# Attention and two feed-forward blocks on one core: planner prices for the later blocks, w_in's first chunk in another place, w_out asked for later, sums of the last pass freed from its scale

## The chip, the cores and the metric

The kernel runs on one core of a Trainium2 chip. The metric is the device time of one execution in microseconds (us). TensorE does the matrix products, VectorE and ScalarE the elementwise work and the evacuation of PSUM, GpSimd some elementwise sums, and SyncE (SP) asks for all transfers.

## The reference

```python
# q, k, v: [4, 8, 768, 64] f32; mem_k, mem_v: [4, 8, 8, 64]
for c in range(24):                       # chunks of 32 queries
    ctx = rows c*32-16 .. c*32+32+8       # cut at both ends of the sequence
    k_full, v_full = concat(mem, ctx)
    s = q_c @ k_full.T / 8
    out[c] = softmax(s) @ v_full          # sum + 1e-9 below
x = out.transpose(0, 2, 1, 3).reshape(3072, 512)
h = x @ w_in                              # 512 x 2048
g = max(h, 0) + alpha * min(h, 0)
y = g @ w_out                             # 2048 x 512
result = ((y @ w_a) * (y @ w_b)) @ w_o2   # 512 x 1536 twice, 1536 x 512
```

The weights come as 64-bit floats, the rest as 32-bit.

## The kernel before, in words

The tokens are cut into 24 attention units of 128 tokens. Seven blocks follow: two of two units (256 tokens), then five of four units (512 tokens). For each block the kernel computes attention into `x32`, finds its largest size, forms a scale by powers of two (`scale`), and splits x into a high and a low 16-bit half (`split_hi` on ScalarE, L347; `split_lo` on VectorE, L351) in `xhl`. A product of two split operands is three 16-bit products (`gemm3`, L910 to L912). `gemm1` makes 16 tiles of g and splits them into `ghl`, `gemm2` makes four tiles of y and stores them to `yd` in HBM.

The weights are turned from words of 64-bit floats into 32-bit floats by bit operations on VectorE (`chunk`, L537 to L560, with an absolute value on ScalarE, L531), scaled and split. w_in comes in eight chunks of 256 columns, with one scale for all of them (`scale_w1`: the maximum over all chunks at L495, the result `s_w1`). Its raw words lie in places that are free then: chunk 0 in the place of `xhl`, chunks 1 to 3 in that of `ghl`, the rest in that of w_out's halves. w_out comes in eight chunks of 64 columns, whose raw words take turns in the three places of `raw_slots`. w_a, w_b and w_o2 come in six chunks each (a "pair" chunk); they are summed into the seven operands of a two-by-two fast product, split, and written to HBM (`spill`).

x's scale (`x_block`, L877 finds the block's largest value) reads s_w1, because one of the two products formed behind it, `iy`, contains w_in's inverse scale.

The second half (`second`) runs six passes of 512 tokens. A pass computes y's two products for six pairs of columns by seven products each (`pair`, `quarters`), multiplies them, and takes the largest size (`amp`). When all six pairs are done, one scale is formed over them (L1253 to L1258), `operands` makes the four sums of each pair's product (`sums`, L367, on GpSimd, or on VectorE in the last pass), splits the seven operands, and `output` makes two tiles of tokens by seven products over all six pairs.

The order of the work is a plan. Every instruction group is put into a list with `sd.op(engine, cost, rank, ...)`: its engine (or a choice of engines), its price in us (`dve`, `act`, `pe`, `pool`, `dma`, or numbers), a rank, and the tiles it reads and writes. `Schedule.emit` then simulates the engines with these prices: at each step it takes the group that can start first, the lower rank where two can start at the same time, and issues it. Each engine and SP's queue then keep that order on the chip, whatever the real durations are. Places (`Slots`) are given out in the same simulation; unless a class of places is marked otherwise, its users take places in the order in which they were declared. An attention unit's transfers have the rank twice its number (unit 3, the fourth, has 6.0), w_out's chunks 4.1, 4.6, 5.1 and so on.

Of the kernel before, what the change touches and what calls it, by code (L numbers as in the profile page):

```python
# [172 lines left out]

def dve(n, rate=1.04, pointers=0):
# [16 lines left out]
def tile_attention_moe_moe2(  # L191
# [28 lines left out]
    TB = 512  # L220
    EARLY = 8
# [82 lines left out]
    def scale(amax, s, inv, reads, writes, rank=-2000, after=()):  # L304


        ps = Buf(mm_slots)

        def across():
            nc.tensor.transpose(out=ps.tile[:, :P], in_=amax().to_broadcast([P, P]), identity=ident)  # L310

        m = Buf(m_slots)

        def largest():
            nc.vector.tensor_reduce(out=m.tile, in_=ps.tile[:, :P], axis=AX.X, op=ALU.max)
# [12 lines left out]
        sd.op("PE", pe(P, 2), -9000, across, reads, [(ps, 0)])  # L328
        sd.op("DVE", dve(P), rank, largest, [(ps, 0)], [(m, 0)])
        sd.op("DVE", 0.07, rank, power, [], [(m, 0)])  # L330
        sd.op("DVE", 0.07, rank, inverse, [(m, 0)], [(m, 1)])
        last = [(m, 2)] if after else writes
        sd.op("DVE", 0.09, rank, itself, [(m, 1)], last)
        for i, fn in enumerate(after):
            sd.op("DVE", 0.07, rank, fn, [(m, 2 + i)], writes if i == len(after) - 1 else [(m, 3 + i)])
# [139 lines left out]
    in_x, in_g = Buf(xhl_slots), Buf(ghl_slots)  # L475
# [4 lines left out]
    def raw_tile(c):  # L480
        if c < 4:
            t = (in_g if c else in_x).tile.rearrange("p x k t -> p (x k t)")
            c = max(0, c - 1)
# [21 lines left out]
    def chunk(nm, c, w, kt, cw, rank, load_rank):  # L505
# [7 lines left out]
        am, s, inv = (s_w1, s_w1, inv_w1) if nm == "w1" else (col(), col(), col())  # L513
# [56 lines left out]
        def after():  # L570
            if nm == "w2":
                r = slice(c % 2 * CR, (c % 2 + 1) * CR)
                nc.vector.tensor_copy(out=inv_w2[r, c // 2 : c // 2 + 1], in_=inv[r])
            else:
                nc.vector.tensor_copy(out=inv_w[nm][:, c : c + 1], in_=inv)
# [14 lines left out]
        if nm != "w1":  # L590
# [3 lines left out]
                rank=rank - 0.3, after=[after],  # L594
# [66 lines left out]
    def attention(iu, b, u, x32, part, am, rank):  # L661
# [163 lines left out]
        for j in range(2):  # L825
# [3 lines left out]
            "PE", 0.3 + 4 * pe(KW, 4) + (0.35 if early else 0.0), prank, scores,  # L829
# [7 lines left out]
        sd.op("ACT", 8 * act(KW, 2) + 0.3, rank, exps, [(sm, "m")] + [(ps, 0)] * early, [(sm, 0)])  # L837
        sd.op("DVE", 0.07, rank, sums, [(sm, 0)], [(sm, 2)])
        sd.op("DVE", 0.09, rank, part_of, [], [(sm, 2)])
        for o in range(2):  # L840
            sd.op(
                None, {"DVE": dve(n), "ACT": 4 * act(KW, 1) + 0.15}, rank, lambda e, o=o: norm(e, o),
# [4 lines left out]
        sd.op("PE", 0.3 + 8 * pe(64, 4), prank, values, [(vw, 0), (pT, 0), (pT, 1)], [(px, 0)], holds=[x32])  # L847
# [8 lines left out]
    t = 0  # L856
# [9 lines left out]
    def x_block(jb, x32, xhl, c0, rank):  # L866
# [9 lines left out]
        def largest():  # L876
# [3 lines left out]
            "DVE", 0.1, rank, largest, [(x32, ("am", p0 + i)) for i in range(nu)], [(f"amx{jb}", 0)]  # L880
# [79 lines left out]
    def gemm2(jb, m, ghl, c0, n, iy, rank):  # L960
# [25 lines left out]
        for i in range(4):  # L986
# [8 lines left out]
            [(f"sx{jb}", 0)] + [(f"inv_w2{2 * m + i}", 0) for i in range(2)], [("iym", jb, m)],  # L995
# [39 lines left out]
    for c in range(NR):  # L1035
        chunk("w2", c, w_out, KF1, CR, 5 + c, 4.1 + 0.5 * c)
# [9 lines left out]
    for jb, (x32, xhl, ghl, c0, ar, r1, r2) in enumerate(place):  # L1046
        n = blocks[jb][1] * P
# [151 lines left out]
    def second(jb, r):  # L1199
# [40 lines left out]
        sd.op("DVE", 0.1, r, largest_y, [(f"amy{jb}", kk) for kk in range(KK)], [(f"amy1{jb}", 0)], late=3.0)  # L1240
# [14 lines left out]
        sd.op("DVE", 0.1, r, largest, [("amp", jb, j) for j in js], [(f"amp1{jb}", 0)], late=0.0 if last_ else 3.0)  # L1255
# [124 lines left out]
```

## Time and profile before

| | us |
|---|---|
| median of 3 runs | 1192.36 |
| lowest and highest | 1191.29, 1195.16 |
| the profiled execution | 1191.92 |
| its span, first to last instruction | 1190.2 |
| TensorE busy in it | 1126.7 |
| VectorE busy | 868.6 |
| ScalarE busy | 604.7 |
| GpSimd busy | 226.5 |

The span is one execution recorded by the profiler. PE is TensorE's matrix products, DVE is VectorE, ACT is ScalarE, POOL is GpSimd, and SPq is SP's queue issuing transfers. A line such as L351 is a line of the kernel; where a helper issues the instruction, it is the helper's line. The names of tiles are shown without their numbers, so that `w` can be w1, w2 or w32.

### The profile page before, as it was taken

What the parts mean: (1) busy time and instruction counts of PE and PEld (TensorE: products, weight loads), DVE (VectorE), ACT (ScalarE), POOL (GpSimd) and SP (SyncE); (2) the same over time, 40 slices, a digit from 0 to 9 for tenths busy, and PEclk for the clock granted to TensorE, in tenths of its full rate; (3) what the DMA queues carried; (4) which work ended last, traced back from release to release, by engine and by line L of the source; (5) the groups of instructions that cost most, each with busy time, mean ns of one, the idle gap of its engine ahead of it and who ended that gap; (6) DMA issues with size and microseconds to landing.
All of it is one profiled execution on the core that took longest, in us unless ns stands there. A gap on an engine that the chain in (4) does not pass through costs nothing.

```text
span 1190.2 us, 23137 instructions
## 1 busy us (share of the span) xinstructions
PE 1126.7 (95%) x9304; PEld 811.2 (68%) x9304; DVE 868.6 (73%) x1533; ACT 604.7 (51%) x1326; POOL 226.5 (19%) x293
## 2 busy tenths in 40 slices
PE   4399999999999999999999999999999999999988
PEld 3278886555445554444444588888888888888877
DVE  6989998987998799335243187886867958858881
ACT  4689778975886698246253032433424423324340
POOL 1000012111112212100300010242433414234130
PEclk9589999999999999899999999999999999999999
DMA  9935664647635633530103052512513514315101
GB/s 263 258 81 139 154 191 127 186 132 219 200 103 167 194 127 106 179 140 32 50 10 133 27 190 90 188 66 94 191 54 112 173 37 156 130 52 187 63 36 37
DMA packets 162523, 150.93 MB, mean 127 GB/s; under 512 B 104032, under 2 KB 139888, under 8 KB 162416
## 3 DMA queue, kind: packets, MB, share of 16 engines
q1 hardware_dynamic: 162416, 149.45, 41.5%
q8 instruction: 73, 1.20, 0.4%
q14 instruction: 34, 0.28, 0.1%
HBM read 120.33 MB, written 29.10 MB: 126 GB/s over the span
## 4 chain that ended last, share of the span: by engine, by line
PE 74%; DVE 13%; ACT 6%; DMA 3%; SPq 2%; issue 2%; ACTq 0%; DVEq 0%
PE mm L910 23%; PE mm L912 23%; PE mm L911 23%; ACT sm L766 2%; PE pair L792 2%; DVE ghl L942 1%; DVE g L933 1%; DVE w L553 1%; PE mm L806 1%; DMA qt<-in_q_dram 1%; SPq L688 1%; DVE nm L756 1%; DVE w L560 1%; ACT sp L347 1%; ACT t L930 1%
## 5 line engine op out<-in xcount | busy, mean ns | idle before, releaser
L912 PE MATMUL mm<-xhl,w 128*128 128x512 f16 (+1 forms) x448 | 157.3, 351 | 1.9 <-DVE w L553 1.9
L910 PE MATMUL mm<-xhl,w 128*128 128x512 f16 (+1 forms) x448 | 157.6, 352 | 0.3 <-ACT t L930 0.2
L912 PE MATMUL mm<-ghl,w 128*128 128x512 f16 (+1 forms) x448 | 156.9, 350 | 0.9 <-DVE w L351 0.9
L911 PE MATMUL mm<-xhl,w 128*128 128x512 f16 (+1 forms) x448 | 157.4, 351 | 0.3 <-DVE xhl L351 0.3
L910 PE MATMUL mm<-ghl,w 128*128 128x512 f16 (+1 forms) x448 | 157.2, 351 | 0.0
L911 PE MATMUL mm<-ghl,w 128*128 128x512 f16 (+1 forms) x448 | 156.9, 350 | 0.0
L910 PE MATMUL mm<-units,w1b 128*128 128x256 f16 x560 | 153.4, 274 | 0.0
L911 PE MATMUL mm<-units,w1b 128*128 128x256 f16 x560 | 153.4, 274 | 0.0
L912 PE MATMUL mm<-units,w1b 128*128 128x256 f16 x560 | 153.3, 274 | 0.0
L912 PEld LDWEIGHTS <-w 128*128 128x128 f16 x896 | 88.2, 98 | 83.5 <-DVE w L553 2.2
L910 PEld LDWEIGHTS <-w 128*128 128x128 f16 x896 | 88.5, 99 | 75.5 <-issue 0.8
L911 PEld LDWEIGHTS <-w 128*128 128x128 f16 x896 | 88.3, 99 | 73.5 <-issue 1.7
L910 PE MATMUL mm<-w2b,w1b 128*128 128x256 f16 x504 | 137.4, 273 | 0.1
L912 PE MATMUL mm<-w2b,w1b 128*128 128x256 f16 x504 | 137.4, 273 | 0.0
L911 PE MATMUL mm<-w2b,w1b 128*128 128x256 f16 x504 | 137.4, 273 | 0.0
L910 PEld LDWEIGHTS <-w1b 128*128 128x128 f16 x1064 | 104.4, 98 | 13.0 <-DMA w1b<-wb_d 0.5
L911 PEld LDWEIGHTS <-w1b 128*128 128x128 f16 x1064 | 104.4, 98 | 12.7
L912 PEld LDWEIGHTS <-w1b 128*128 128x128 f16 x1064 | 104.4, 98 | 12.2
L367 POOL TENSOR_TENSOR raw<-w 128x256 f32<-128x256 f32 x18 | 16.1, 893 | 409.7 <-ACT raw L568 248.8
L933 DVE SCALAR_TENSOR_TENSOR g<-t,columns,g 128x512 f32<-128x512 f32 (+1 forms) x112 | 75.8, 683 | 24.3 <-ACT t L930 24.2
L942 DVE TENSOR_TENSOR ghl<-g,ghl 128x512 f16<-128x512 f32 (+1 forms) x112 | 70.8, 638 | 23.8 <-ACT ghl L939 23.4
L927 ACT ACTIVATE g<-mm 128x512 f32<-128x512 f32 (+1 forms) x112 | 60.5, 547 | 50.5 <-PE mm L912 48.4
(293 smaller groups left out, 2403.5 us busy)
## 6 DMA issues: line engine op xcount, KB each, us to landing
w1b<-wa_d SPq DMA_DIRECT2D x26, 896.0 KB
w1b<-wb_d SPq DMA_DIRECT2D x26, 896.0 KB
raw<-in_moe_w_out_dram SPq DMA_DIRECT2D x8, 1024.0 KB
kw<-in_k_dram SPq DMA_DIRECT2D x40, 176.0 KB
vw<-in_v_dram SPq DMA_DIRECT2D x40, 176.0 KB
qt<-in_q_dram SPq DMA_DIRECT2D x24, 256.0 KB
raw<-in_moe_w_a_dram SPq DMA_DIRECT2D x12, 512.0 KB
raw<-in_moe_w_b_dram SPq DMA_DIRECT2D x12, 512.0 KB
```

Of the source, the lines that this page charges most:

```text
L347: nc.scalar.activation(out=hi, in_=src, func=ACTF.Copy, scale=s)
L367: (nc.vector if e == "DVE" else nc.gpsimd).tensor_tensor(out=out_()[:, i], in0=x()[:, a], in1=y()[:, b], op=op)
L553: nc.vector.scalar_tensor_tensor(out=f, in0=lo, scalar=29, in1=f, op0=ALU.logical_shift_right, op1=ALU.bitwise_or)
L560: nc.vector.scalar_tensor_tensor(out=lo if nm == "w1" else f, in0=hi, scalar=KEEP, in1=f, op0=ALU.bitwise_and, op1=ALU.bitwise_or)
L766: nc.scalar.activation(out=sm.tile[:, o, g], in_=scored()[:, o, g], func=ACTF.Exp, bias=stat["nm"][:, i : i + 1], scale=1.0, accum_out=sta ...
L792: nc.tensor.transpose(out=heads(pp, P)[:KW, o, g], in_=sm.tile[:, o, g], identity=ident)
L910: nc.tensor.matmul(out=ps, lhsT=lh, rhs=rh, start=first and i == 0, stop=False)
L911: nc.tensor.matmul(out=ps, lhsT=lh, rhs=rl, start=False, stop=False)
L912: nc.tensor.matmul(out=ps, lhsT=ll, rhs=rh, start=False, stop=last and i == n - 1)
L927: nc.scalar.activation(out=g.tile[:, :n], in_=ps.tile[:, :n], func=ACTF.Relu, scale=E1)
L933: nc.vector.scalar_tensor_tensor(out=g.tile[:, :n], in0=t2.tile[:, :n], scalar=nal[:, m : m + 1], in1=g.tile[:, :n], op0=ALU.mult, op1=ALU ...
L942: nc.vector.tensor_tensor(out=ghl.tile[:, 1, m, d], in0=g.tile[:, :n], in1=ghl.tile[:, 0, m, d], op=ALU.subtract,)
```

## The change

1. The planner gets two tables of prices. `SHORT` holds the prices as they were. `FULL` has larger ones: 0.15 and 0.17 us instead of 0.07 and 0.06 before the first column on VectorE and ScalarE, 0.57 instead of 0.357 us for one exp, 0.42 instead of 0.267 for one scaled row group, but 0.9 instead of 1.16 us for the scores and 1.15 instead of 2.02 for the values. It holds for the attention and the gemms of blocks 3 to 6 (`EXACT = 3`) and for the conversion of w_a, w_b and w_o2; the second half is planned with `SHORT`.
2. Chunk 0 of w_in lies in a place of `raw_slots`, which it takes first, and no longer in that of `xhl`.
3. x's scale doesn't read s_w1; `iy` is formed by an operation of its own that does.
4. w_out's chunks have the ranks 6.1, 6.6 and so on.
5. A pair chunk's inverse scale is written where it is needed at once, without a copy.
6. In the last pass a pair's sums wait for its own product and its `amp` and not for the scale; the first two pairs put their sums of three into places of `p32_slots` instead of `s32_slots`, and the operands of the first two pairs (not the last two) lie in `yu_slots`, the other four in `ring_slots`.

```diff
+SHORT = dict(
+    dve=0.07, act=0.06, rate=0.833, tiny=0.07, itself=0.09, part=0.09, largest=0.1,
+    exp=0.357, scaled=0.267, scores=1.16, values=2.02,
+)
+FULL = dict(
+    dve=0.15, act=0.17, rate=0.85, tiny=0.15, itself=0.16, part=0.2, largest=0.2,
+    exp=0.57, scaled=0.42, scores=0.9, values=1.15,
+)
 def dve(n, rate=1.04, pointers=0):
-    return 0.07 + 0.06 * pointers + n * rate / 1000
+    return took["dve"] + 0.06 * pointers + n * rate / 1000
 def act(n, pointers=0):
-    return 0.06 + 0.09 * pointers + n * 0.833 / 1000
+    return took["act"] + 0.09 * pointers + n * took["rate"] / 1000
...
-    in_x, in_g = Buf(xhl_slots), Buf(ghl_slots)
+    in_x, in_g = Buf(raw_slots), Buf(ghl_slots)
...
-        am, s, inv = (s_w1, s_w1, inv_w1) if nm == "w1" else (col(), col(), col())
+        am, s, inv = (s_w1, s_w1, inv_w1) if nm == "w1" else (col(), col(), inv_w[nm][:, c : c + 1] if pair else col())
...
-        sd.op("ACT", 8 * act(KW, 2) + 0.3, rank, exps, [(sm, "m")] + [(ps, 0)] * early, [(sm, 0)])
+        sd.op("ACT", 8 * took["exp"], rank, exps, [(sm, "m")] + [(ps, 0)] * early, [(sm, 0)])
...
-
-            lambda: nc.vector.tensor_tensor(out=iy, in0=inv, in1=iy0, op=ALU.mult),
         ]
         scale(
-            lambda: am1, s, inv, [(f"amx{jb}", 0), ("alpha", 0), ("s_w1", 0)], [(f"sx{jb}", 0)], after=after
+            lambda: am1, s, inv, [(f"amx{jb}", 0), ("alpha", 0)], [(f"sx{jb}", 0)], after=after
+        )
+        sd.op(
+            "DVE", took["tiny"], rank, lambda: nc.vector.tensor_tensor(out=iy, in0=inv, in1=iy0, op=ALU.mult),
+            [(f"sx{jb}", 0), ("s_w1", 0)], [(f"iy{jb}", 0)],
         )
...
-        chunk("w2", c, w_out, KF1, CR, 5 + c, 4.1 + 0.5 * c)
+        chunk("w2", c, w_out, KF1, CR, 5 + c, 6.1 + 0.5 * c)
...
+        took.update(SHORT if jb < EXACT else FULL)
...
-    def operands(r, b, h, s, reads, cost):
-        o = Buf(s32_slots)
+    def operands(r, b, h, s, reads, cost, ready=None, slots_=None):
+        o = Buf(slots_ or s32_slots)
         unit = lambda: b.tile
-        others = lambda: o.tile
-        sd.op("POOL", 0.0, r, lambda: None, reads, [(h, "held")], holds=[h])
+        others = lambda: o.tile[:, :3]
+        sd.op("POOL", 0.0, r, lambda: None, reads if ready is None else ready, [(h, "held")], holds=[h])
...
-        pu = {j: Buf((ring_slots if i < 4 else yu_slots) if last_ else pu_slots) for i, j in enumerate(js)}
+        pu = {j: Buf((yu_slots if i < 2 else ring_slots) if last_ else pu_slots) for i, j in enumerate(js)}
...
-            operands(r, ps[j], pu[j], lambda j=j: spj[:, j : j + 1], [(f"sp{jb}", 0), (ps[j], 0)], cost)
+            operands(
+                r, ps[j], pu[j], lambda j=j: spj[:, j : j + 1], [(f"sp{jb}", 0), (ps[j], 0)], cost,
+                [(ps[j], 0), ("amp", jb, j)] if last_ else None,
+                p32_slots if last_ and j in list(js)[:2] else None,
+            )
```

## Rows read from the trace of the kernel before

**Rows 1.** The page: busy time, and the granted clock in 40 slices of 29.8 us

```profile
PE 1126.7 (95%) x9304; PEld 811.2 (68%) x9304; DVE 868.6 (73%) x1533; ACT 604.7 (51%) x1326; POOL 226.5 (19%) x293
...
PEclk9589999999999999899999999999999999999999
```

**Rows 2.** Windows: length, busy us of PE, PEld, DVE, ACT, POOL; granted clock, DMA, GB/s

```profile
200.00:300.00 100.00, 97.01 (x840) 54.45 (x839) 86.47 (x154) 75.23 (x190) 14.54 (x20) 1.00 0.58 165
300.00:400.00 100.00, 94.00 (x771) 52.40 (x770) 86.90 (x163) 77.07 (x206) 16.55 (x20) 1.00 0.59 166
400.00:500.00 100.00, 96.19 (x651) 48.93 (x650) 78.34 (x135) 67.94 (x152) 22.15 (x21) 0.97 0.42 137
470.00:480.00 10.00, 6.74 (x103) 4.57 (x98) 9.30 (x16) 6.25 (x11) 1.21 (x1) 0.85 0.75 197
480.00:490.00 10.00, 10.00 (x66) 4.71 (x65) 4.26 (x18) 2.82 (x4) 2.15 (x4) 0.81 0.24 96
1150.00:1160.00 10.00, 5.45 (x38) 3.68 (x36) 8.61 (x12) 3.95 (x4) 3.47 (x4) 0.81 0.14 52
1160.00:1170.00 10.00, 10.00 (x80) 8.41 (x78) 1.72 (x3) 0.47 (x1) 0.00 (x0) 0.85 0.01 2
```

**Rows 3.** Waits of TensorE in 200:500: us in total, times, longest

```profile
PE mm L806 <- DVE columns L815: 2.5, 1, 2.5
PE pair L792 <- DVE sm L782: 2.0, 3, 1.0
...
PE pair L740 <- ACT kT L647: 1.5, 1, 1.5
```

**Rows 4.** Timeline of VectorE, 42:62: start, us, engine, line, operation

```profile
42.56 0.15 DVE L877 TENSOR_REDUCE columns<-columns 128x1 f32<-128x2 f32 x1
...
48.64 0.15 DVE L495 TENSOR_REDUCE columns<-columns 128x1 f32<-128x8 f32 x1
...
52.38 0.28 DVE L315 TENSOR_REDUCE m<-mm 128x1 f32<-128x128 f32 x1
...
53.73 1.29 DVE L351 SCALAR_TENSOR_TENSOR w<-xhl,columns,w 128x1024 f16<-128x1024 f32 x1 [0.23 <-ACT w L347]
...
57.64 1.42 DVE L351 SCALAR_TENSOR_TENSOR xhl<-x,columns,xhl 128x512 f16<-128x512 f32 x2 [0.24 <-ACT xhl L347]
```

**Rows 5.** Timeline of ScalarE, 51.6:58

```profile
52.49 1.20 ACT L347 ACTIVATE w<-xhl,columns 128x1024 f16<-128x1024 f32 x1 [1.04 <-DVE w L560]
```

**Rows 6.** Timeline of TensorE, 58:61.5

```profile
60.24 1.09 PE L705 MATMUL mm<-ident,qt 128*128 128x128 f32 x4 [10.33 <-DMA qt<-in_q_dram]
61.12 0.42 PE L910 MATMUL mm<-xhl,w 128*128 128x256 f16 x1
```

**Rows 7.** Timeline of SP's queue, 41:56

```profile
41.61 7.23 SPq L469 DMA_DIRECT2D raw<-in_moe_w_out_dram  x3
48.94 3.50 SPq L688 DMA_DIRECT2D kw<-in_mem_k_dram  x1
```

**Rows 8.** Groups by line and form on ScalarE in 200:480: busy us, mean ns

```profile
L766 ACT ACTIVATE sm<-sm,nm 128x96 f32<-128x96 f32 x112 | 40.3, 363 | 15.5 <-DVE nm L756 15.4
...
L766 ACT ACTIVATION_READ_ACCUMULATOR sm<-sm,nm 128x1 f32 x113 | 21.4, 189 | 0.0
```

**Rows 9.** The chain that ended last, 300:306: start, us, what

```profile
302.80 2.98 ACT sm L766 x16
```

**Rows 10.** Timeline of VectorE, 1127:1160

```profile
1132.77 0.23 DVE L1257 TENSOR_SCALAR columns<-columns 128x6 f32<-128x6 f32 x1
...
1158.40 1.01 DVE L351 SCALAR_TENSOR_TENSOR units<-s,columns,units 128x768 f16<-128x768 f32 x1
```

**Rows 11.** Timeline of GpSimd, 1100:1160

```profile
1134.13 0.72 POOL L367 TENSOR_TENSOR quarters<-quarters 128x256 f32<-128x256 f32 x1 [17.60 <-DVE s L367]
```

**Rows 12.** Timeline of TensorE, 1152.6:1159

```profile
1156.42 0.39 PE L912 MATMUL mm<-units 128*128 128x256 f16 x1 [3.25 <-DVE units L351]
...
1158.54 0.39 PE L912 MATMUL mm<-units 128*128 128x256 f16 x1 [1.30 <-DVE units L351]
```

More of the change, by code (lines that the diff above doesn't have):

```diff
@@ L220, in tile_attention_moe_moe2 @@
     TB = 512
+    EXACT = 3
     EARLY = 8
@@ L329, in scale @@
         sd.op("DVE", dve(P), rank, largest, [(ps, 0)], [(m, 0)])
-        sd.op("DVE", 0.07, rank, power, [], [(m, 0)])
-        sd.op("DVE", 0.07, rank, inverse, [(m, 0)], [(m, 1)])
+        sd.op("DVE", took["tiny"], rank, power, [], [(m, 0)])
+        sd.op("DVE", took["tiny"], rank, inverse, [(m, 0)], [(m, 1)])
         last = [(m, 2)] if after else writes
-        sd.op("DVE", 0.09, rank, itself, [(m, 1)], last)
+        sd.op("DVE", took["itself"], rank, itself, [(m, 1)], last)
         for i, fn in enumerate(after):
-            sd.op("DVE", 0.07, rank, fn, [(m, 2 + i)], writes if i == len(after) - 1 else [(m, 3 + i)])
+            sd.op("DVE", took["tiny"], rank, fn, [(m, 2 + i)], writes if i == len(after) - 1 else [(m, 3 + i)])
     def to_float(m):
@@ L480, in raw_tile @@
     def raw_tile(c):
+        if c == 0:
+            return in_x.tile
         if c < 4:
-            t = (in_g if c else in_x).tile.rearrange("p x k t -> p (x k t)")
-            c = max(0, c - 1)
+            t, c = in_g.tile.rearrange("p x k t -> p (x k t)"), c - 1
         else:
@@ L570, in after @@
         def after():
[L571 to L575, printed above, removed]
+            r = slice(c % 2 * CR, (c % 2 + 1) * CR)
+            nc.vector.tensor_copy(out=inv_w2[r, c // 2 : c // 2 + 1], in_=inv[r])
         sd.op("SP", dma(n * 8 * P), load_rank, load, (), [rk])
@@ L593, in chunk @@
                 lambda: am, s, inv, [(key + "am", 0)], [(key + "s", 0), (f"inv_{nm}{c}", 0)],
-                rank=rank - 0.3, after=[after],
+                rank=rank - 0.3, after=[after] if nm == "w2" else [],
             )
@@ L828, in attention @@
         sd.op(
-            "PE", 0.3 + 4 * pe(KW, 4) + (0.35 if early else 0.0), prank, scores,
+            "PE", took["scores"] + (0.35 if early else 0.0), prank, scores,
             [(qT, 0), (kT, 0), (kT, 1)], [(ps, 0)],
@@ L836, in attention @@
             sd.op("DVE", dve(2 * n), rank, largest, [(sm, 0)], [(sm, "m")])
-        sd.op("ACT", 8 * act(KW, 2) + 0.3, rank, exps, [(sm, "m")] + [(ps, 0)] * early, [(sm, 0)])
-        sd.op("DVE", 0.07, rank, sums, [(sm, 0)], [(sm, 2)])
-        sd.op("DVE", 0.09, rank, part_of, [], [(sm, 2)])
+        sd.op("ACT", 8 * took["exp"], rank, exps, [(sm, "m")] + [(ps, 0)] * early, [(sm, 0)])
+        sd.op("DVE", took["tiny"], rank, sums, [(sm, 0)], [(sm, 2)])
+        sd.op("DVE", took["part"], rank, part_of, [], [(sm, 2)])
         for o in range(2):
             sd.op(
-                None, {"DVE": dve(n), "ACT": 4 * act(KW, 1) + 0.15}, rank, lambda e, o=o: norm(e, o),
+                None, {"DVE": dve(n), "ACT": 4 * took["scaled"]}, rank, lambda e, o=o: norm(e, o),
                 [(sm, 2), (sm, 0)], [(sm, ("n", o))],
@@ L846, in attention @@
             sd.op(None, either(512), rank, lambda e, o=o: p_evac(e, o), [(pp, o)], [(pT, o)])
-        sd.op("PE", 0.3 + 8 * pe(64, 4), prank, values, [(vw, 0), (pT, 0), (pT, 1)], [(px, 0)], holds=[x32])
+        sd.op("PE", took["values"], prank, values, [(vw, 0), (pT, 0), (pT, 1)], [(px, 0)], holds=[x32])
         sd.op(None, either(512), rank, x_evac, [(px, 0)], [(x32, part)])
@@ L879, in x_block @@
         sd.op(
-            "DVE", 0.1, rank, largest, [(x32, ("am", p0 + i)) for i in range(nu)], [(f"amx{jb}", 0)]
+            "DVE", took["largest"], rank, largest, [(x32, ("am", p0 + i)) for i in range(nu)], [(f"amx{jb}", 0)]
         )
@@ L994, in gemm2 @@
             "DVE", 0.07, rank - 1000, evac_scale,
-            [(f"sx{jb}", 0)] + [(f"inv_w2{2 * m + i}", 0) for i in range(2)], [("iym", jb, m)],
+            [(f"iy{jb}", 0)] + [(f"inv_w2{2 * m + i}", 0) for i in range(2)], [("iym", jb, m)],
         )
@@ L1055, in tile_attention_moe_moe2 @@
             chunk(nm, c, w, 0, 0, 1000 + c, 1000 + c)
+    took.update(SHORT)
     ring_slots, yu_slots, pu_slots, w3_slots, p32_slots = (Slots(0, None) for _ in range(5))
@@ L1238, in largest_y @@
             nc.vector.tensor_reduce(out=am1y, in_=am, axis=AX.X, op=ALU.max)
-        sd.op("DVE", 0.1, r, largest_y, [(f"amy{jb}", kk) for kk in range(KK)], [(f"amy1{jb}", 0)], late=3.0)
+        sd.op("DVE", took["largest"], r, largest_y, [(f"amy{jb}", kk) for kk in range(KK)], [(f"amy1{jb}", 0)], late=3.0)
         after = [
@@ L1253, in largest @@
             nc.vector.tensor_reduce(out=am1, in_=amp, axis=AX.X, op=ALU.max)
-        sd.op("DVE", 0.1, r, largest, [("amp", jb, j) for j in js], [(f"amp1{jb}", 0)], late=0.0 if last_ else 3.0)
+        sd.op("DVE", took["largest"], r, largest, [("amp", jb, j) for j in js], [(f"amp1{jb}", 0)], late=0.0 if last_ else 3.0)
         after = [
```

1 line of the change is left out of this document (added).

## The prediction

> **What bounds the kernel now.** I read the page first. TensorE is busy 95% of the span and VectorE 73% [rows 1]: the end moves only where TensorE stands still or runs at the lower clock. The clock line [rows 1] shows such places at the start, around 480 us and at the end.
>
> Then the windows by stage, for those places. In 200:500 TensorE is idle 300 - 97.01 - 94.00 - 96.19 = 12.8 us; in 470:490 the granted clock is 0.85 and 0.81, which costs another 10 x 0.15 + 10 x 0.19 = 3.4 us; in 1150:1160 it is idle 4.55 us, and the low clock of that slice and the next costs 1.9 + 1.5 = 3.4 us [rows 2]. (Full clock is 2.4 GHz, the lower level 1.2.) Between 500 and 1150 there is next to nothing to win. The waits in 200:500 name small stalls on the softmax chain, each up to 1.5 us, and one of 2.5 us behind a `values` product [rows 3].
>
> Last the timelines of the two ends. The first product of gemm 1 starts at 61.12 us [rows 6]. What ends last before it is VectorE, not the load that the wait names: VectorE turns w_in's words into floats until the maximum over w_in (L495, 48.64), then comes the scale of x (L315, 52.38), the low half of w_in's chunk 0 (53.73) and only at 57.64 the low halves of x, which end at 59.06 [rows 4]. The transposition of q that then waits for its load starts at 60.24 [rows 6], 1.2 us behind that.
>
> **The change part by part.** Its own sums stand against the profiled execution, 1191.92 us (span 1190.2 and 1.7 around it); the median of the three runs is 0.4 us above that.
>
> *Start.* Block 0's maximum (L877) is there at 42.56 [rows 4], but today its scale also reads s_w1, and xhl is held by w_in's chunk 0 until that is split. Both go. So the scale (from L315 at 52.38 to before the low half at 53.73, 1.35 us) and the low halves of x (1.42 us) [rows 4] move in front of L495. They are no less work: they push the end of s_w1 back by 1.4 + 1.4 = 2.8 us. Behind it today lie chunk 0's high half (52.49, 1.20 us) [rows 5] and low half (53.73 to 55.02) [rows 4]. With x ready, the first product can start at 55.02 + 2.8 = 57.8 less the 1.35 us of x's scale that no longer stand in between, so 56.5 to 57.8 against 61.12: 3.3 to 4.6 us. TensorE will first run at the lower clock as it does now, and VectorE still has to make the low halves of the chunks that follow, of which some are made by then today (the 57.64 of x stands behind them [rows 4]); I take 3.0. Bounds: 0 if TensorE then waits for those low halves as long as it gained, 6.1 (61.12 - 55.02) if VectorE had gaps for the whole of x.
>
> The w_out chunks: three issues held SP for 7.23 us from 41.61, and the fourth unit's k could not be asked for before 48.94 [rows 7]. Now its k, q and v go first, and w_out's chunks behind them. Queued behind w_out on SP is then the fifth unit, about where it is now, since the same bytes stand ahead of it. In its first pass w_out has two places instead of three until chunk 0 is split, but VectorE gets to w_out only after w_in. So I cost this at 0, under cover of VectorE's work on w_in; if the cover is gone, it is the 7.2 us of issue.
>
> The copy of each pair's inverse scale, 18 times one column on VectorE (nearest row: L877, one column from two, 0.15 us [rows 4]; 18 x 0.15 = 2.7 us), goes; it lies under gemm products: 0. The iy product only changes its wait: 0.
>
> *Middle.* From the fourth block on the planner has dearer prices. Nothing is added to the engines; the order changes on all of them, the DMA issues too. The trace shows what kind of price the new ones are: one exp is 363 ns and its read of the sum 189 ns [rows 8], together the 0.57 of the new table, times 8 = 4.56 us. But the 16 pieces of a unit pass in 2.98 us [rows 9], near the old 2.86: the durations overlap. So the new plan believes ScalarE and VectorE slower than they are, and places TensorE's part of attention later behind them; in the run the operands then lie ready. The Trainium skill, "ScalarE: Activation LUTs", What ACT_TABLE_LOAD costs, says that back-to-back ACTIVATEs overlap by about 93 ns; an estimate from it, 4.4 - 15 x 0.093 = 3.0 us, agrees with the row, and speaks against durations as prices.
>
> What can be won are the stalls of the softmax chain. I take the rows up to 2.0 in total each as gone (2.0 + 1.5 [rows 3], and as much again in their shorter neighbours, 7 in all), half of the 2.5 + 3.4 us around 480 us [rows 2, 3], and 4 us of new stalls, since every order leaves some: 7 + 3 - 4 = 6.0 gained. Bounds: 16.2 (12.8 + 3.4, all of it) and a loss of as much as the new table overstates (below).
>
> *End.* In the last pass the four sums of each pair's product now wait only for that product and its maximum, not for the scale over all six. The scale is ready at 1132.77; the last low half starts at 1158.40 and ends at 1159.4 [rows 10], and TensorE stands 3.25 and 1.30 us for it [rows 12]. GpSimd was idle for 17.6 us until 1134.13 [rows 11]: room for the sums, 4 x 0.72 = 2.9 us per pair there [rows 11]. But their places: two come from the big ring only when the last pair has its place, two are the old ones. So four of six pairs can be summed before the scale, and the other two wait for a place until a pair is split. Behind the scale are left 12 high and 12 low halves; the low ones end at about 1.0 us for the small ones [rows 10] and 1.29 for the big ones [rows 4], 6 x 2.3 = 13.8 us, and with nine evacuations of the output before them (about 5 us, an estimate from x's low half of 512 columns, 0.71 us, and half of that for 256 [rows 4]) and one pair's sums on VectorE (about 1.5 us by the same estimate; the other pair's on GpSimd) they fill VectorE from 1133 to about 1155. TensorE needs the last big one at about 1153 and the small one 2 us later. So of 4.55 + 3.4 = 8.0 us [rows 2] I take 6.5 as gained, a stall of a microsecond as left. Bounds: 0 (the two late pairs take as long as all six) and 8.0.
>
> Sum: 1191.9 - 3.0 - 6.0 - 6.5 = 1176.4; on the median's level 1176.9, **1177 us**.
>
> **Rivals.**
>
> 1. *Only the end pays.* VectorE is the bound of the first 100 us, so an earlier start runs into it, and the new order has as many stalls as the old: 1192.4 - 6.5 - 1 = 1185. For it: VectorE's rows before the first product follow each other with hardly a gap [rows 4]; against: TensorE's share over the span [rows 1] leaves no room for long waits elsewhere, so what starts earlier mostly runs on.
>
> 2. *The middle pays nearly whole:* 1192.4 - 3 - 14 - 7 = 1168. For it: no engine but TensorE is full there.
>
> 3. *The other side: slower, by deferred attention.* Each of the 16 units from the fourth block on has exps priced 4.56 - 2.98 = 1.6 us too dear. If the plan lets TensorE's order wait for that, so that x of a block comes late and gemm 1 stands, it costs up to 16 x 1.6 = 25 us; it decides where it eats the 9.5 us of the two ends, from 9.5 / 16 = 0.6 us a unit on; at full price 1192.4 - 9.5 + 25 = 1208. Against it: gemm 2 of the block before is there to fill, and VectorE is busy 0.87 in the middle [rows 2]. The overlap that the ScalarE page of the Trainium skill states is the reason behind this rival.
>
> 4. *It does not do what it says:* the two late pairs hold the end, w_out's delay eats the start, the middle comes out even: 1189 to 1195, about 1191.
>
> **How the numbers follow.** Forecast 0.45 (1171 to 1183), rival 1 0.22, rival 2 0.13, rival 3 0.08, rival 4 0.12. The measurement tells 0.3% (3.6 us) from no change, so faster is under 1188.8: 0.45 + 0.22 + 0.13 and a quarter of rival 4, 0.83; same 0.09, slower 0.08. The range leaves out rival 3, most of rival 4 and the lower edge of rival 2: 1167 to 1189.
>
> **What would show it.** Start: x's low halves before L495, and the first gemm 1 product at 57 us, not 61; the fourth unit's loads ahead of w_out's. Middle: idle TensorE in 200:500 at 7 us instead of 12.8, and the clock at 1.00 around the last unit. End: sums on GpSimd before the last scale, a stall of a microsecond or less, the clock at 1.00. I am wrong if gemm 1 starts early but then waits for low halves of w_in, if stalls of over a microsecond recur in the middle, or if the last pairs' sums still stand behind the scale.

## The result, and the profile after

The changed kernel takes 1163.42 us (median of 4 runs, 1162.94 to 1164.01) against 1193.76 us for the kernel before on the same chip: a ratio of 0.9748, 95% interval 0.9727 to 0.9769. Faster, as predicted, but by 30 us and not by 15: below the range. In lines after the change, `gemm3` is L925 to L927, `split_hi` L361, `split_lo` L365, `sums` L381.

The page of the kernel after, busy time and granted clock [rows 1]:

```profile
PE 1116.2 (96%) x9304; PEld 808.8 (70%) x9304; DVE 874.9 (75%) x1524; ACT 595.5 (51%) x1300; POOL 232.3 (20%) x298
...
PEclk8599999999999999999999999999999999999999
```

Only the start still runs at the lower clock level. To see where the time went, I cut both traces at three products: the first of gemm 1, the first of block 2's gemm 1 (the first `128x512` on `xhl`), and the first of a pair in the second half (`units`, `w1b`). The stretches between, for the kernel before and then after (columns as in [rows 2]):

```profile
61.00:182.90 121.90, 117.14 (x1295) 100.19 (x1294) 112.40 (x247) 100.20 (x289) 3.83 (x4) 0.97 0.56 138
182.90:680.20 497.30, 484.51 (x3242) 247.31 (x3240) 328.32 (x572) 297.69 (x692) 72.54 (x84) 0.99 0.41 127
680.20:1190.20 510.00, 500.30 (x4547) 445.48 (x4545) 379.92 (x631) 172.81 (x264) 145.20 (x164) 0.99 0.33 109
```

```profile
58.80:178.80 120.00, 112.87 (x1283) 97.30 (x1281) 112.51 (x241) 97.47 (x275) 0.00 (x0) 0.99 0.60 147
178.80:658.00 479.20, 479.20 (x3242) 246.67 (x3240) 339.64 (x575) 295.41 (x682) 76.70 (x88) 1.00 0.43 131
658.00:1161.30 503.30, 497.57 (x4547) 444.46 (x4545) 377.68 (x626) 172.71 (x264) 150.65 (x169) 1.00 0.34 110
```

The span fell by 28.9 us: 2.3 before gemm 1, 1.8 in the early stage (blocks 0 and 1), **18.1 in the middle** and 6.7 in the second half. The middle has 3242 recorded products before and after. Its 12.8 us of idle TensorE went to nothing, and 5.3 us of busy time went too (484.51 to 479.20). So the records show no idle time there that another order could still win (a gap shorter than the overlap of two recorded products would not show). The windows that answer to [rows 2] say the same:

```profile
200.00:300.00 100.00, 100.00 (x858) 56.55 (x857) 82.08 (x137) 71.42 (x182) 14.23 (x16) 1.00 0.55 153
300.00:400.00 100.00, 100.00 (x793) 54.66 (x792) 82.74 (x144) 71.55 (x178) 15.66 (x20) 1.00 0.58 168
400.00:500.00 100.00, 100.00 (x693) 51.88 (x692) 82.89 (x147) 68.45 (x164) 18.39 (x20) 1.00 0.39 118
470.00:490.00 20.00, 20.00 (x126) 10.09 (x125) 15.94 (x28) 10.30 (x28) 3.35 (x4) 1.00 0.65 215
```

*The start.* VectorE's timeline after [rows 4]: start, us, line.

```profile
42.49 0.15 DVE L889 TENSOR_REDUCE columns<-columns 128x1 f32<-128x2 f32 x1
...
46.05 1.41 DVE L365 SCALAR_TENSOR_TENSOR xhl<-x,columns,xhl 128x512 f16<-128x512 f32 x2 [0.18 <-ACT xhl L361]
...
52.55 0.15 DVE L510 TENSOR_REDUCE columns<-columns 128x1 f32<-128x8 f32 x1
...
55.96 0.55 DVE L794 TENSOR_TENSOR sm<-sm,rs 128x384 f32<-128x384 f32 x1
57.25 1.28 DVE L365 SCALAR_TENSOR_TENSOR w<-raw,columns,w 128x1024 f16<-128x1024 f32 x1 [0.74 <-ACT w L361]
```

And TensorE's [rows 6]:

```profile
56.66 1.06 PE L804 MATMUL pair<-ident,sm 128*96 128x128 f32 x4 [2.98 <-DVE sm L794]
57.51 1.48 PE L728 MATMUL pair<-ident,kw 96*128 96x96 f32 x8
58.79 0.42 PE L925 MATMUL mm<-xhl,w 128*128 128x256 f16 x1
```

x's low halves are at 46.05 instead of 57.64, ahead of the maximum over w_in (52.55, was 48.64). The first product starts at 58.79, behind an attention unit's transposition (L804) that waits for VectorE's softmax (L794) and one of k (L728).

*The end.* GpSimd's timeline [rows 11], with the last scale for comparison (VectorE) and the one stall of TensorE that is left [rows 12]:

```profile
1092.42 1.44 POOL L381 TENSOR_TENSOR w2b<-quarters 128x256 f32<-128x256 f32 x1
...
1121.67 1.64 POOL L381 TENSOR_TENSOR s<-xhl 128x256 f32<-128x256 f32 x1 [13.79 <-DVE w1b L365]
```

```profile
1110.62 0.23 DVE L1276 TENSOR_SCALAR columns<-columns 128x6 f32<-128x6 f32 x1
...
1131.72 1.00 DVE L365 SCALAR_TENSOR_TENSOR w1b<-s,columns,w1b 128x768 f16<-128x768 f32 x1
```

```profile
1131.85 0.28 PE L927 MATMUL mm<-units,w1b 128*128 128x256 f16 x1 [0.66 <-DVE w1b L365]
```

The last pass's sums begin 18 us ahead of the scale at 1110.62; the late pairs begin at 1121.67 on GpSimd, after 13.79 us of idle time that ends with a low half of VectorE's (a place that comes free); a stall of 0.66 us is left.

### The profile page after: what moved, and what is told of

Its sections match the earlier page's. It is cut to its first block, busy times and chain, and to the rows that moved or that the text cites. A ratio compares the mean times of both kernels' runs of the same rounds, so it can differ in the third digit from the quotient of the medians.

```text
span 1161.3 us, 23129 instructions
## 1 busy us (share of the span) xinstructions
PE 1116.2 (96%) x9304; PEld 808.8 (70%) x9304; DVE 874.9 (75%) x1524; ACT 595.5 (51%) x1300; POOL 232.3 (20%) x298
## 4 chain that ended last, share of the span: by engine, by line
PE 87%; DVE 7%; ACT 3%; DMA 1%; issue 1%; POOL 0%; SPq 0%; ACTq 0%; DVEq 0%; POOLq 0%
PE mm L925 27%; PE mm L927 27%; PE mm L926 26%; PE pair L804 2%; PE mm L818 2%; PE pair L728 1%; PE pair L752 1%; DVE w L568 1%; DMA w1b<-wb_d 1%; PE mm L717 1%; DVE w L365 1%; ACT sm L778 1%; DVE w L575 0%; DMA kw<-in_k_dram 0%; PE mm L324 0%
## 5 line engine op out<-in xcount | busy, mean ns | idle before, releaser
L927 PE MATMUL mm<-ghl,w 128*128 128x512 f16 (+1 forms) x448 | 156.2, 349 | 2.5 <-DVE w L365 2.5
L925 PE MATMUL mm<-xhl,w 128*128 128x512 f16 (+1 forms) x448 | 156.7, 350 | 1.3 <-ACT t L945 1.2
L925 PE MATMUL mm<-ghl,w 128*128 128x512 f16 (+1 forms) x448 | 156.3, 349 | 0.3 <-ACT w L361 0.3
L927 PE MATMUL mm<-xhl,w 128*128 128x512 f16 (+1 forms) x448 | 156.5, 349 | 0.0
L927 PE MATMUL mm<-units,w1b 128*128 128x256 f16 x560 | 152.6, 273 | 0.7 <-DVE w1b L365 0.7
L925 PE MATMUL mm<-units,w1b 128*128 128x256 f16 x560 | 152.6, 273 | 0.0
L927 PEld LDWEIGHTS <-w 128*128 128x128 f16 x896 | 87.8, 98 | 83.1 <-DVE w L365 3.4
L925 PEld LDWEIGHTS <-w 128*128 128x128 f16 x896 | 87.9, 98 | 75.0 <-ACT w L361 0.5
L925 PE MATMUL mm<-w2b,w1b 128*128 128x256 f16 x504 | 137.4, 273 | 0.3 <-DMA w1b<-wb_d 0.2
L927 PE MATMUL mm<-w2b,w1b 128*128 128x256 f16 x504 | 137.4, 273 | 0.0
L927 PEld LDWEIGHTS <-w1b 128*128 128x128 f16 x1064 | 104.1, 98 | 13.1 <-DVE w1b L365 0.9
L925 PEld LDWEIGHTS <-w1b 128*128 128x128 f16 x1064 | 104.1, 98 | 12.9 <-DMA w1b<-wb_d 0.8
L381 POOL TENSOR_TENSOR raw<-w 128x256 f32<-128x256 f32 x18 | 15.3, 852 | 456.7 <-ACT raw L583 456.7
```

The source lines that it names most:

```text
L381: (nc.vector if e == "DVE" else nc.gpsimd).tensor_tensor(out=out_()[:, i], in0=x()[:, a], in1=y()[:, b], op=op)
L925: nc.tensor.matmul(out=ps, lhsT=lh, rhs=rh, start=first and i == 0, stop=False)
L927: nc.tensor.matmul(out=ps, lhsT=ll, rhs=rh, start=False, stop=last and i == n - 1)
```

## The experiments

"After" is the changed kernel, with 1163.42 us; a ratio is always to the kernel before on the same chip. That kernel took 1192.1 to 1194.3 us on the chips of these runs, so compare ratios where times are close. The table gives the cuts named above, in us of the span: first product of gemm 1, first of block 2, first of a pair, and the length of the middle between the last two.

| kernel | time | ratio, 95% interval | gemm 1 | block 2 | pair | middle |
|---|---|---|---|---|---|---|
| before | 1193.76 | 1 | 61.1 | 182.9 | 680.2 | 497.3 |
| after | 1163.42 | 0.9748 (0.9727 to 0.9769) | 58.8 | 178.8 | 658.0 | 479.2 |
| no table | 1186.91 | 0.9953 (0.9935 to 0.9970) | 58.9 | 181.9 | 681.5 | 499.6 |
| table alone | 1178.62 | 0.9873 (0.9857 to 0.9890) | 58.9 | 191.5 | 667.2 | 475.6 |
| place alone | 1197.12 | 1.0035 (1.0023 to 1.0047) | 57.0 | 193.8 | 684.8 | 491.0 |
| x waits again | 1171.11 | 0.9812 (0.9783 to 0.9840) | 57.3 | 185.8 | 665.7 | 479.8 |
| old w_out ranks | 1180.72 | 0.9890 (0.9857 to 0.9923) | 57.2 | 197.6 | 673.4 | 475.8 |
| end undone | 1170.13 | 0.9810 (0.9789 to 0.9832) | 58.9 | 178.9 | 658.2 | 479.2 |
| TensorE's prices only | 1170.80 | 0.9822 (0.9796 to 0.9848) | 58.8 | 178.9 | 664.9 | 485.9 |
| the others' only | 1165.59 | 0.9774 (0.9753 to 0.9795) | 59.1 | 179.8 | 661.1 | 481.3 |
| conversion as before | 1164.80 | 0.9756 (0.9729 to 0.9783) | 59.9 | 179.9 | 660.0 | 480.1 |
| half the surcharge | 1170.98 | 0.9818 (0.9800 to 0.9836) | 58.7 | 179.2 | 664.7 | 485.6 |
| double | 1166.03 | 0.9781 (0.9761 to 0.9801) | 59.0 | 179.4 | 660.9 | 481.5 |
| gemm products 12% cheaper | 1174.44 | 0.9851 (0.9831 to 0.9872) | 59.1 | 182.3 | 669.6 | 487.3 |
| fixed margin, 1.5 us | 1177.78 | 0.9864 (0.9835 to 0.9894) | 59.1 | 180.5 | 673.7 | 493.2 |
| fixed margin, 4 us | 1179.70 | 0.9888 (0.9873 to 0.9903) | 59.1 | 179.8 | 673.5 | 493.7 |
| dear from block 0 | 1194.55 | 1.0010 (1.0000 to 1.0019) | 58.1 | 215.2 | 690.6 | 475.4 |
| and old w_out ranks | 1194.54 | 1.0013 (1.0000 to 1.0025) | 61.4 | 213.9 | 689.3 | 475.4 |
| and all conversion dear | 1193.46 | 1.0013 (0.9995 to 1.0030) | 62.2 | 215.7 | 691.1 | 475.4 |
| dear from block 2 | 1180.51 | 0.9910 (0.9882 to 0.9938) | 58.9 | 198.2 | 674.3 | 476.0 |

Where the middle is 475 or 476, some 85 products have moved in front of block 2 (3157 or 3158 in the middle instead of 3242), with the place alone 101, without the table and with cheaper gemm products 16: of such a row, read the pair column, which holds both. Two orders with the same prices in the middle differ little in it: 497.3 and 499.6 us with the old prices, 479.2 and 479.8 with the table (after, x waits again).

**Is it the table?** First the changed kernel without it.

```diff
-    EXACT = 3
+    EXACT = 7
```

> The changed kernel with the old prices throughout (no block planned with the dear table). If the dear table made the gain in the middle, the 18.0 us between gemm 1 of block 2 and the first pair product come back, about 1181 us, with idle TensorE of some 13 us in 200:500. If the earlier start or the other parts made it, about 1165 us.

The middle is 499.6 us, no better than before. The waits of TensorE in it (us in total, times, longest) and its window:

```profile
PE mm L324 <- ACT raw L583: 9.5, 10, 1.6
PE mm L324 <- DVE columns L889: 2.3, 2, 1.9
PE pair L752 <- ACT kT L659: 1.8, 1, 1.8
```

```profile
181.90:681.50 499.60, 482.60 (x3226) 245.29 (x3224) 330.05 (x556) 300.13 (x694) 75.43 (x85) 1.00 0.41 126
```

The stalls are not softmax alone: ten times TensorE stands at the transposition in `scale` (L324) for ScalarE's step of the conversion of w_a, w_b and w_o2 (L583), each up to 1.6 us. The after trace has no wait at all from 179 to 658. Nor does the table act at the start: with and without it the instructions of every engine come in the same order up to 166 us.

The other way round: the kernel before with the two price tables (in the place of w_in's first chunk, x's wait, w_out's ranks and the last pass it is the kernel before; it keeps two small edits, the operation of its own for `iy` and item 5).

> The kernel before with the two price tables alone: neither the first chunk's place, nor the free scale of x, nor w_out's later ranks, nor the fifth place at the end. If the middle's gain is the table's own work, the stretch from block 2's first product to the first pair product is about 480 us (497 before), the end and the start stay as before, and the time is 1192 - 17 = about 1175 us. If the middle needs the other parts (w_out's place in the queue, x's scale), it stays at 490 or more and the time is 1185 to 1193 us.

1178.62: the first pair product is 13.0 us earlier than before, 667.2. Without table and start parts it was 680.2, with the start parts alone (no table) 681.5, with both 658.0. So the start parts are worth -1.3 us on the old prices and 9.1 us on the new; the table is worth 13.0 without them (the two small edits counted with it, since no run has them alone) and 23.5 with them. The parts do not add up; each redraws the order that the next one meets.

**What in the table works?** Two halves of it, each alone:

```diff
-FULL = dict(dve=0.15, act=0.17, ..., scores=0.9, values=1.15)
+FULL = dict(SHORT, scores=0.9, values=1.15)                        # TensorE's prices only
+FULL = dict(dve=0.15, act=0.17, ..., scores=1.16, values=2.02)     # the others' only
```

> From block 3 on only TensorE's prices of the scores and the values are changed (0.9 and 1.15 us), ScalarE and VectorE keep the old ones. Theory P (dear prices of ScalarE and VectorE give TensorE's waits a margin): no gain in the middle, about 1181 us. Theory Q (TensorE was priced 1.13 us a unit too slow, so it ran ahead of the plan): about 1164 us.

> From block 3 on ScalarE and VectorE have the dear prices, the scores and the values keep the old 1.16 and 2.02 us. Theory P: about 1164 us, TensorE without idle time in 200:500. Theory Q: about 1181 us, the stalls of the kernel before.

485.9 and 481.3: either half takes most of it. Making TensorE cheaper and making the others dearer does the same to the plan: it changes their ratio. TensorE's old prices were not true either. In the kernel before, from 180 to 650 us, the values and the scores, 32 products a unit each, took

```profile
L806 PE MATMUL mm<-pT,vw 96*64 96x64 f32 x512 | 19.0, 230 | 3.3 <-DVE columns L815 2.5 <-DMA vw<-in_v_dram 0.8
...
L740 PE MATMUL pair<-kT,qT 64*64 64x96 f32 x480 | 13.7, 249 | 1.5 <-ACT kT L647 1.5
```

which is 1.19 and 0.91 us a unit where the old prices were 2.02 and 1.16. Then the conversion's prices alone set back, before the loop over w_a, w_b and w_o2:

```diff
+    took.update(SHORT)
```

> The blocks from the fourth on keep the dear prices; the conversion of w_a, w_b and w_o2 has the old ones. With all prices old, 9.5 us of 17 us of idle TensorE in 180:500 were waits of the conversion's scale for ScalarE. If the conversion's prices give these waits their margin: about 1173 us, with these waits back. If the blocks' prices do: about 1164 us.

480.1: they hardly matter. Next, the size: VectorE's and ScalarE's surcharge halved (`exp=.4635`, `dve=.11`, ...) or doubled (`exp=.783`, `dve=.23`, ...), with the old prices for scores and values.

> From the fourth block on half of the table's surcharge on ScalarE and VectorE; the scores and the values keep their old prices. With the whole surcharge the stage takes 481.3 us, with none 499.6. By a rate of the engines that is set right step by step, about 490 us, 1174 in all; if any surcharge redraws the order into a good one, 481; if it is the luck of one order, either side.

> Twice the table's surcharge on ScalarE and VectorE from the fourth block on, old prices of the scores and the values. If the surcharge only has to be large enough, the middle stage stays at 479 to 481 us: 1164. If it defers attention when it is too large, as in the first blocks, the stage grows to 490 us or more: 1173 and up.

None 499.6, half 485.6, full 481.3, double 481.5: a gain that saturates, next to the 479.2 of the kernel after. It takes no exact price. Nor, for ScalarE, a true one: `exp` at 0.57 is far above what an exp takes in these runs (0.36 us from one to the next with its read), and at 0.783 it is further still. A price that is false on the other side, gemm products 12% too cheap and all else as in `SHORT`:

```diff
-FULL = dict(...)
+FULL = dict(SHORT, gemm=0.88)
...
-            "PE", KD * pe(n, 3), rank, product,
+            "PE", took["gemm"] * KD * pe(n, 3), rank, product,
```

> All prices old, but from the fourth block on gemm 1 and gemm 2 count 12% less on TensorE, which is false. If the ratio of the rates in the plan is what counts, the middle stage falls from 499.6 to 480 to 486 us: 1164 to 1170 us. If true prices are what counts, it stays at 495 to 500 us: 1182 to 1187.

487.3, with 6.9 us of the L583 waits left. Last, the old prices and a fixed margin: in the plan, TensorE's groups of the conversion and from block 3 on wait 1.5 us (then 4 us) beyond the end of each operand that another engine makes.

```diff
-                x.ready = max(x.ready, o.end + lag + o.late)
+                x.ready = max(x.ready, o.end + lag + o.late + (x.margin if e != "PE" else 0.0))
...
```

> Old prices throughout, but in the plan an instruction group on TensorE, of the blocks from the fourth on and of the conversion, counts as ready 1.5 us after what it waits for on ScalarE or VectorE. If the dear table works as a margin in front of TensorE's waits, this does the same without any dearer load: about 1165 us, the middle stage (gemm 1 of block 2 to the first pair product) near 481 us. If it works by making the load of ScalarE and VectorE what it is, the stage stays near the 499.6 us of old prices: 1187 us.

> Old prices, and a margin of 4 us in the plan instead of 1.5 in front of TensorE's groups that wait for ScalarE or VectorE. If margin is what counts and 1.5 us (stage of 493 us, 6.5 us gained) was too little, the stage comes to 481 us, 1166 us in all. If the two engines fall behind the plan by rate, without end, a fixed margin does not get there: 488 us or more, 1173 and up.

493.2 and 493.7: a third of the gain, and no more for more margin. But the stalls are not the same ones. With 1.5 us there are still 6.5 us of waits for the conversion (L584 there); with 4 us these are gone, and two long waits of products make up most of its 10.2 us of idle time:

```profile
PE mm L926 <- ACT qT L725: 4.0, 1, 4.0
PE mm L926 <- DVE g L992: 2.7, 1, 2.7
```

So a margin in front of TensorE's operands alone does not do what the prices do. That the plan must let the other engines lag behind TensorE by a share of their work, so that on the chip they are ahead of it, fits all these runs; no run measures that lag.

**Why not from the first block?** The same table from block 0 on, then with w_out's old ranks, then with the conversion of w_in and w_out dear too, then from block 2 on:

```diff
-    EXACT = 3
+    EXACT = 0            # from block 0; the two runs after it have this too
+        chunk("w2", c, w_out, KF1, CR, 5 + c, 4.1 + 0.5 * c)   # the first of them
+    took.update(FULL)    # the second, at the start
+    EXACT = 2            # from block 2, alone
```

> The dear table for the blocks 0 to 2 as well (w_in and w_out keep the old prices). If wrong rates between the engines are what leaves stalls, those of the stage from the first gemm 1 product to gemm 1 of block 2 go too (idle 6 to 7 us of 120): about 1157 us. If VectorE bounds that stage (19.8 and 19.7 of 20 us busy in 80:120), nothing is gained: 1163 us or a few more.

> As the run with the dear table for all blocks, but w_out's chunks with the old ranks. With the old prices in the first blocks these ranks cost 17 us, in stalls at 140 to 185 us. If those stalls are an order redrawn by a plan with wrong rates, the dear prices heal most of it: within 5 us of the run with the new ranks. If the early w_out chunks really take places or transfers from attention, 10 us or more are lost again.

> The dear table from the very first group on, so for the conversion of w_in and w_out too. If the first blocks lost 37 us because attention was dear and the conversion beside it cheap, the stage comes back to about 120 us: 1160 us. If dear prices as such defer attention where no long gemm 2 fills, it stays at 150 us or so: 1190 us.

> The dear table from block 2 on, the first block of four units. Its attention runs beside the gemms of the blocks of two. If the loss lies in the two short blocks, the time stays at 1163 us or gains 1 or 2; if it lies in attention that runs before the first long gemm 2, some 10 us are lost: 1173 us.

The middle stays as good, but the pair column is 31 to 33 us later than after, and 16 us later with block 2. The longest wait ends 16 to 17 us ahead of block 2's first product each time; here from block 2 on, around 175 us, ScalarE, VectorE and TensorE:

```profile
172.08 2.54 ACT L361 ACTIVATE xhl<-x,columns 128x512 f16<-128x512 f32 x4
176.69 0.38 ACT L778 ACTIVATE sm<-sm,nm 128x96 f32<-128x96 f32 x1 [2.07 <-DVE nm L768]
...
179.57 1.13 ACT L361 ACTIVATE w<-w,columns 128x1024 f16<-128x1024 f32 x1
181.25 1.17 ACT L800 ACTIVATE sm<-sm,rs 128x96 f32<-128x96 f32 x4 [0.54 <-DVE rs L789]
```

```profile
173.00 2.73 DVE L365 SCALAR_TENSOR_TENSOR xhl<-x,columns,xhl 128x512 f16<-128x512 f32 x4
175.72 0.94 DVE L768 TENSOR_REDUCE nm<-sm 128x8 f32<-128x768 f32 x1
...
178.26 1.23 DVE L568 SCALAR_TENSOR_TENSOR w<-raw,w 128x1024 int32<-128x1024 int32 x1
```

```profile
172.23 0.32 PE L324 MATMUL mm<-ident,columns 128*128 128x128 f32 x1 [1.53 <-ACT raw L583]
181.89 1.06 PE L804 MATMUL pair<-ident,sm 128*96 128x128 f32 x4 [9.34 <-ACT sm L800]
```

x of block 2 is split at 175.73, and of block 1's gemm 2 there are 96 products left, which run without a wait later. But the plan has put a unit's transposition (L804) in front of them, and that waits for the whole softmax: the maximum (L768), eight exps, weight work that both engines do in between (L568, L361), the normalization (L800). TensorE stands 9.34 us; the rest of the 16 us is shorter waits and the granted clock, 0.87 in 160:200. Why the plan put it there is not shown. The longest wait of the three runs with dear prices from block 0 on is of the same kind, 6.7, 6.8 and 7.8 us, but it is only a part of their loss. Between the first products of gemm 1 and of block 2, with dear prices from block 0 on:

```profile
58.10:215.20 157.10, 132.46 (x1377) 110.14 (x1378) 130.03 (x267) 109.46 (x309) 2.83 (x4) 0.88 0.49 120
```

TensorE is idle for 24.6 us there, against 7.1 after; the rest is the lower granted clock (0.88 against 0.99) and 94 products more.

**The start's parts.** x's scale made to read s_w1 again; then w_out's old ranks; then, on the kernel before, the first chunk's place and nothing else.

```diff
-    [(f"amx{jb}", 0), ("alpha", 0)]
+    [(f"amx{jb}", 0), ("alpha", 0), ("s_w1", 0)]      # x waits again
```

```diff
-        chunk("w2", c, w_out, KF1, CR, 5 + c, 6.1 + 0.5 * c)
+        chunk("w2", c, w_out, KF1, CR, 5 + c, 4.1 + 0.5 * c)      # old w_out ranks
```

```diff
-    in_x, in_g = Buf(xhl_slots), Buf(ghl_slots)
+    in_x, in_g = Buf(raw_slots), Buf(ghl_slots)      # place alone, on the kernel before
```

> x's scale reads w_in's scale again; chunk 0 stays in its new place, w_out behind the fourth unit. If the earlier split of x is what made gemm 1 start 2.3 us earlier, it starts at 61 us again and the time is 1165.7 us. If w_out's later request did, gemm 1 still starts at 59 us and the time is 1163.4.

> w_out's chunks have the old ranks 4.1 and on; all else as changed. If the order of the loads was covered by VectorE's work, as predicted, no change: 1163.4 us. If the fourth unit's late load would now hold TensorE in front of gemm 1 (its transposition of q stands ahead in the order), gemm 1 starts at 61 us or later: 1166 us.

> The kernel before with w_in's first chunk in a place of raw words and nothing else. If the place alone frees x's low halves at the start, the first product of gemm 1 comes at about 57 us instead of 61, and, if that is kept, the time is 1188 to 1190 us. If the place frees nothing, 61 us and 1192 us. If the start is gained and the order of the first blocks eats it, 57 us at the first product and 182 us or later at block 2's first product.

With x waiting again the first product is not later but earlier, at 57.3, and the kernel is 7.7 us slower all the same. The longest of TensorE's waits from 40 to 186 there, 6.2 us for the high half of x, ends with that first product. The loss is behind it, 8.5 us up to block 2, in waits such as

```profile
PE mm L324 <- ACT raw L583: 4.5, 2, 3.9
PE mm L927 <- DVE w L561: 1.8, 1, 1.8
PE mm L927 <- DVE w L568: 1.1, 1, 1.1
```

and in a granted clock of 0.95 instead of 0.99 over that stretch. With w_out's old ranks the first product is at 57.2 as well, but its third then waits 1.97 us for the low half of w_in's chunk, until 59.83 (after: 59.22); and 15.4 us are lost up to the first pair product, in waits of the same kind as above (60 to 198 us):

```profile
PE pair L804 <- ACT sm L800: 5.3, 1, 5.3
PE pair L804 <- DVE sm L794: 3.4, 1, 3.4
```

The place alone gives 57.0, the earliest of all, and makes the kernel before 0.35% slower: block 2's first product comes 10.9 us later than before, with 101 products more in front of it, and the first pair product 4.6 us.

**The end undone:** in the last pass the sums wait for the scale again, with the old places.

```diff
-        pu = {j: Buf((yu_slots if i < 2 else ring_slots) if last_ else pu_slots) for i, j in enumerate(js)}
+        pu = {j: Buf((ring_slots if i < 4 else yu_slots) if last_ else pu_slots) for i, j in enumerate(js)}
...
-                [(ps[j], 0), ("amp", jb, j)] if last_ else None,
-                p32_slots if last_ and j in list(js)[:2] else None,
+                None, None,
```

> The sums of the last pass wait for the scale again, with the places as before; all else as changed. If the end's gain is from the sums in front of the scale, 6.7 us come back: 1170 us, with a stall of 4 to 5 us before the last output and the clock below 1.00 behind it. If the end gained from the order in front of it, 1164 us.

Up to the first pair product nothing changes (658.2); the second half is 509.2 us instead of 503.3, and the stalls of [rows 12] are back:

```profile
PE mm L927 <- DVE units L365: 4.9, 2, 3.2
```

## Why the prediction was right and wrong

The sum predicted 1176.9 on the median's level and 1163.4 was measured. Of the 13.5 us between, the middle is 12.1, the early stage, which had no term of its own, 1.8, the end 0.2, less 0.7 at the start.

**The middle: the step that failed.** It took 6.0 us: 7 of softmax stalls, "half of the 2.5 + 3.4 us around 480 us", and "4 us of new stalls, since every order leaves some". It measured 18.1. The order left no stall at all, so the 4 us, for which no row stood, were wrong, and so was the half. The sum also took the new prices as dearer throughout, though two of TensorE's fell; those two alone take 13.7 us of the 20.4 between no table and after. The upper bound, 16.2 for "all of it", was itself too low by 1.9 us: 5.3 us of busy time went beside the 12.8 of idle time, and the low clock around 480 us was put at 3.4 of them. TensorE's timeline of the kernel after, at 300 us, suggests what the rest is:

```profile
300.03 0.38 PE L926 MATMUL mm<-xhl,w 128*128 128x512 f16 x1
300.24 0.38 PE L927 MATMUL mm<-xhl,w 128*128 128x512 f16 x1
```

Products of 0.38 us start 0.21 to 0.22 us apart, so they overlap in the records by 0.16, and across a stall that overlap is missing. The 15 stalls that the waits list in the middle before make 15 x 0.16 = 2.4 us, near the 1.9. Five kernels bear it out that run the middle with 3241 to 3243 products and show no stretch of 10 us there below a clock of 1.00 (TensorE's prices only, the others' only, half, double, the margin of 1.5 us): their 39 listed stalls come with 8.6 us more busy time than after has, 0.22 each. So a stall costs its idle time and about 0.2 us more. (The kernel without the table can't be read so: it has 16 products fewer in the middle, and its granted clock, 1.00 as a mean, dropped after one of its stalls:)

```profile
311.90:331.90 20.00, 18.10 (x134) 8.71 (x133) 17.68 (x36) 16.63 (x44) 0.00 (x0) 0.91 0.57 155
```

The mechanism was half right. "The new plan believes ScalarE and VectorE slower than they are [...]; in the run the operands then lie ready" fits the runs, since dear prices of the two and twice as dear ones take nearly all of the gain, and a trace without a wait shows the operands ready. But lower prices of TensorE do most of it too, and the size doesn't grow with the falseness of the price: from the full surcharge on, the gain is nearly all there is. Rival 2 (1168, the middle pays 14) was the nearest, and was still short. Why a fixed margin of 4 us doesn't do the same is not settled.

The Trainium skill's overlap of ACTIVATEs ("ScalarE: Activation LUTs", What ACT_TABLE_LOAD costs) agrees with the rows: in the run from block 2 on, eight exps with their reads pass in 2.88 us (176.69 to 179.57), where the durations of [rows 8] add up to 4.4. It speaks against 0.57 as the time of an exp. It says nothing against it as a price of a plan; the double price shows that.

**Rival 3, deferred attention,** named a loss that exists, and it is where the choice of the fourth block pays: with the table from block 0 on, the loss (31 to 33 us in the first half) eats the whole gain, 1194. I had put it on the 16 units behind the fourth block, at 1.6 us each, and argued that gemm 2 of the block before fills. There it does: no wait from 179 to 658. Ahead of block 2's first product, where VectorE is also converting weights, it does not. Nor is its form the one I gave: x of a block does not come late (block 2's is split at 175.73, its gemm 1 starts at 198.24); products that run without a wait later stand behind a transposition that waits.

**The start: right in size, wrong in its reason.** 2.3 us for the 3.0. x's low halves did move in front of L510, and s_w1's end moved back. But I had misread what ended last in the kernel before: "VectorE, not the load that the wait names". VectorE was done with x at 59.06 [rows 4]; the transposition of q that stands in front of the first product starts only at 60.24 [rows 6], when its load, asked for behind w_out's issues [rows 7], has come. SP's queue before:

```profile
54.91 1.25 SPq L676 DMA_DIRECT2D qt<-in_q_dram  x1
```

The run with the table alone shows the same. VectorE's low halves of x start later there than before (58.27 against 57.64), but the transposition of q stands behind the first twelve products (62.03), and these begin 2.2 us earlier:

```profile
58.89 0.37 PE L924 MATMUL mm<-xhl,w 128*128 128x256 f16 x1 [8.35 <-ACT xhl L361]
59.73 0.37 PE L925 MATMUL mm<-xhl,w 128*128 128x256 f16 x1 [0.47 <-DVE xhl L365]
```

The table has no part in that: the kernels with and without it (after, no table) have the same order up to 166 us. VectorE's order in this run differs from before first at `iy`, which is no longer in x's scale. So "Both go" was not needed for it: this run has neither the place nor the free scale, and the place alone gives 57.0. What ends last before the first product is another thing in each order: q's load before, a unit's transpositions after, x's high half where x waits again, the high half of w_in's chunk with w_out's old ranks. And that product says little of the time: the earliest three of it belong to kernels that are slower than after by 8 to 34 us.

**w_out at 0, under cover: right for the change, wrong for the part.** SP did ask for the fourth unit first, and TensorE never waited for a w_out transfer. But the cover had a hole before, the 1.2 us by which q's load ended behind VectorE, and the part's alternative is not 0: the old ranks cost 17 us in this kernel. I priced the transfers and not the order of all engines that the ranks redraw. The same holds for x's scale, 7.7 us.

**The end: right.** 6.5 predicted, 6.7 in the second half, and 5.9 when undone alone. Four pairs were summed ahead of the scale and two waited for places, as worked out, and the stall "of a microsecond" is 0.66 at a clock of 1.00.

## What to carry to other kernels

In a plan that is simulated from prices, what counted here is the ratio between the bound engine and those that feed it: lean it so that the feeders look slower than they are, sweep that lean (none, half, full, double) until it saturates, and switch it off where it loses, here the blocks beside which VectorE still converts weights. Bound such a change by the idle time of the bound engine in the whole stage plus what each stall costs beside it, and take that bound seriously: an order can win all of it. And don't price a planner's edits one by one, since each is worth what the order around it makes of it: here one part was -1 us or +9, and the earliest start stood in a slower kernel.

## What was not expected of the hardware

A stall costs TensorE more than its recorded idle time: back-to-back 512-column products overlap in the records by 0.16 us, and 39 stalls in five kernels came with 0.22 us more busy time each. And the granted clock stayed at 1.00 through 1130 to 1140 us with the stall of 0.66 us in it, where the two stalls of 3.25 and 1.30 us had left it at 0.81 and 0.85 for two slices [rows 2, 12]:

```profile
1130.00:1140.00 10.00, 9.34 (x86) 8.13 (x85) 4.44 (x7) 0.66 (x2) 0.00 (x0) 1.00 0.14 54
```
